# A pooled attention, a two-of-four expert layer and a gated convolution in one kernel: the tile of mixed heads by three products, and loads, scalings and key projections in another order

## The chip, the cores and the metric

The kernel runs on one NeuronCore of a Trainium2 chip. The metric is the device time of one execution in microseconds (us). Times of different runs of a kernel lie within a per cent here; the profile is of one execution.

## What is computed

Three layers, each in float32. The batch is 4, the sequence 1152, pooled to 576 query positions; 8 heads of 64.

```
q_pool = q.reshape(B, H, S // 2, 2, D).mean(axis=3)
scores = (1 / sqrt(D)) * q_pool @ k.transpose(0, 1, 3, 2)
attn   = softmax(scores)                      # sum + 1e-9
x      = (attn @ v)  as (B, 576, 512)

logits = x @ w_gate                           # 4 experts, the best 2 by softmax
for e in range(4):                            # causal attention of width 64 per expert
    a   = softmax(causal((1 / sqrt(64)) * (x @ wq[e]) @ (x @ wk[e]).T))
    out += weight_of_e * (a @ (x @ wv[e]) @ wo[e])

gate = sigmoid(causal convolution of 5 taps over out)
y    = (gate * (out @ w_val)) @ w_out
```

## The kernel before

**Numbers in two parts.** Where float32 accuracy is wanted of a product in the faster format F32R, an operand x is split into a high part, x rounded to F32R, and a low part, the rest. A product of two split operands needs high x high, low x high and high x low; low x low is left out. `THREE = ((0, 0), (1, 0), (0, 1))` lists these.

**Stage 1, the attention (the first 510 us or so).** The 16 pairs of heads (`pairs`) are worked through one after the other. A pair has two units; unit 0 has four tiles of 128 queries, unit 1 five. The fifth, the mixed tile, (2, 4) in `UNITS`, takes the last 64 queries of both heads at once. For tile m:
- `scores` (line 408): for each of three groups of 384 keys, products into the PSUM tile `s`. In an ordinary tile the stationary operand `qst` has the high parts of 64 query dimensions in the upper partitions and the low parts in the lower; `ka` and `kb` hold the keys of the two heads, each key's dimensions twice over the partitions, as high and as low parts. Two products then give all four terms. In the mixed tile the columns are 64 queries of head 0 and 64 of head 1, with zeros in the other head's place, so that four products per group are wanted: two heads by two parts.
- `rowmin` (413, VectorE), `expo` (419, ScalarE), and, two tiles later, `transp` (457, TensorE), whose results ScalarE and VectorE bring to `pt` (465, 467).
- `shares` (428 to 435): the reciprocals of the sums on VectorE, then their spreading to `rm` on GpSimd. At the end of a unit `av` (470 to 494) transposes `rm` (444, 446), makes the 36 value products (482), and multiplies (484); GpSimd splits the result (491, 487), and a DMA stores it to `x_d` (488).

Ahead of this, `load` fetches a pair's keys `kt`, queries `qt` and values `vn` (344 to 348), and `prep` works over a pair in four portions on GpSimd: the two queries of a pool are added (387, `qp`), the keys cast and subtracted into `hlk` (364, 365), the queries scaled, cast and subtracted (380 to 382). DMAs then move the parts to the partitions in which `scores` wants them (371 for keys, twelve per pair; 375 to 377 for queries, six).

The first pair has its own way in (`first`): its data are loaded twice over the partitions, and the splits are made in place (`kpart`, `qpart`, lines 521 to 530).

**What sets the order.** Everything is written out by hand: each engine runs its instructions in the order of the code. The loop over m calls, in a fixed pattern, `transp` of tile m - 2, `expo` of m, `scores` of m + 1 and one portion of `prep`. Work put on the list `late` is issued one tile later. All DMAs are issued by SyncE, in one queue, in that same order. Behind it in the loop run two generators as background work, from m = 5 on: `dense_weights` (decodes the last layer's weights, a chunk per unit) and `expert_weights` with `folded_weights` (one step per tile). They use VectorE, GpSimd and SyncE.

**Stage 2, the experts (510 to 725 us).** Steps (b, g, i): batch, pair of experts, tile of queries. Between the parts of a step a list `fill` of TensorE work is used up: projections of queries and keys (`proj`, 233), values and gates (`vgate`, 264), the mixing of results, the folding of the last weights (`fold`). `proj` makes queries first (w = 0), then keys (w = 1), two halves each; `move` then copies them to `qs` and `ks` (245 to 250). The convolution's taps (206, VectorE) ride along behind the portions of `fill`; `RD` says at which of five steps the first portion has a rider. **Stage 3** (from 725 us) makes the last products and the output. Its sigmoids need a table of ScalarE, which a dummy activation (`warm`, 951) loads beforehand.

## Time and profile before

| | |
|---|---|
| runs of the kernel | 808.44 us median of 3 (804.37 to 809.11) |
| the profiled execution | 807.51 us, its span 805.7 us |
| TensorE busy | 769.3 us, 95% of the span |
| VectorE, ScalarE, GpSimd busy | 542.0, 473.7, 310.6 us (67%, 59%, 39%) |
| moved by DMA | 134.50 MB, mean 167 GB/s |

The profile is read in stretches, since the stages have different limits. A row of the timeline gives the start and the length of some like instructions in a row, and in brackets how long the engine had been idle before them and what ended that. SPq is SyncE's queue of DMA issues; a row there is the issuing, not the transfer.

### The profile page before, as it was taken

Reading aid. Unit: us, or ns where it says so; the run is one execution under the profiler, and the core shown is the slowest. Engines: PE = TensorE matmul, PEld = TensorE weight load, DVE = VectorE, ACT = ScalarE, POOL = GpSimd, SP = SyncE. Lnnn points to the kernel's source line nnn. Section 1 sums busy time; section 2 is a strip of 40 time slices with the busy share of each in tenths; the row PEclk is TensorE's granted clock in tenths of the full one; section 3 lists DMA queues with packets and bytes.
Section 4 is the critical chain, followed back from the end, with each engine's and each line's share of the span. In section 5 each row is a group of like instructions: output and inputs, shape, how many; then the busy total and the mean of one; then the engine's idle time right before and its main releaser. Section 6 shows DMA issues by size and latency. Waiting matters only on the chain.

```text
span 805.7 us, 14797 instructions
## 1 busy us (share of the span) xinstructions
PE 769.3 (95%) x5348; PEld 627.6 (78%) x5348; DVE 542.0 (67%) x998; ACT 473.7 (59%) x1024; POOL 310.6 (39%) x420
## 2 busy tenths in 40 slices
PE   5889999989999999999999999998999999988998
PEld 4658778767787787787787787887988989877887
DVE  4547877886787777565566566335579899897740
ACT  5547656665676676676566567523455564647532
POOL 3555765757746636525435421112222222230000
PEclk9989999999999999999999999999999999999999
DMA  7778688678787677666565564156465364800112
GB/s 232 155 199 234 152 234 230 183 227 231 226 243 205 194 237 181 179 197 163 163 204 149 168 184 180 44 142 192 89 167 153 92 194 117 265 33 15 66 66 91
DMA packets 86296, 134.50 MB, mean 167 GB/s; under 512 B 21584, under 2 KB 58960, under 8 KB 86224
## 3 DMA queue, kind: packets, MB, share of 16 engines
q1 hardware_dynamic: 86224, 133.57, 58.8%
q8 instruction: 42, 0.69, 0.4%
q14 instruction: 30, 0.25, 0.1%
HBM read 53.37 MB, written 21.76 MB: 93 GB/s over the span
## 4 chain that ended last, share of the span: by engine, by line
PE 71%; DVE 10%; DMA 6%; ACT 4%; SPq 4%; POOL 3%; issue 2%; ACTq 0%; DVEq 0%; POOLq 0%
PE t L482 17%; PE s L408 16%; PE t L457 13%; PE a L233 6%; PE o L998 6%; PE a L264 4%; DVE nm L413 3%; ACT p L419 3%; PE a L788 3%; DMA xh<-x_d 2%; PE s L690 2%; PE a L655 2%; PE a L762 1%; DVE pt L467 1%; SPq L513 1%
## 5 line engine op out<-in xcount | busy, mean ns | idle before, releaser
L465 ACT ACTIVATE pt<-t 128x384 f32<-128x384 f32 x288 | 132.6, 489 | 132.5 <-PE t L457 131.3
L413 DVE TENSOR_REDUCE nm<-s 128x1 f32<-128x1152 f32 x144 | 194.1, 1348 | 23.7 <-PE s L408 17.5
L457 PE MATMUL t<-ident,p 128*128 128x128 f32 x1296 | 205.5, 278 | 2.5 <-ACT pt L465 2.4
L419 ACT ACTIVATE p<-s,nm 128x1152 f32<-128x1152 f32 x144 | 176.0, 1222 | 38.4 <-DVE nm L413 35.8
L457 PEld LDWEIGHTS t<-ident,p 128*128 128x128 f32 x1296 | 151.0, 141 | 43.4 <-issue 13.5
L482 PE MATMUL t<-pt,vn 128*64 128x320 f32 (+1 forms) x1152 | 149.2, 413 | 0.0
L408 PE MATMUL s<-ka,qst 128*128 128x384 f32 x480 | 128.5, 371 | 8.5 <-ACT ka L529 6.8
L408 PE MATMUL s<-kb,qst 128*128 128x384 f32 x480 | 132.4, 368 | 2.2 <-ACT p L419 1.5
L482 PEld LDWEIGHTS t<-pt,vn 128*64 128x64 f32 x1152 | 80.8, 138 | 55.9 <-issue 4.6
L467 DVE COPY pt<-t 128x384 f32<-128x384 f32 x144 | 80.3, 558 | 63.4 <-PE t L457 59.1
L408 PEld LDWEIGHTS s<-ka,qst 128*128 128x128 f32 x480 | 77.9, 193 | 16.7 <-ACT p L419 8.9
L726 POOL TENSOR_TENSOR p<-p,sm 128x512 f32<-128x512 f32 (+3 forms) x32 | 40.1, 1254 | 113.3 <-DVE sm L724 82.1
L408 PEld LDWEIGHTS s<-kb,qst 128*128 128x128 f32 x480 | 77.3, 191 | 5.4 <-ACT p L419 2.1
L484 DVE TENSOR_TENSOR xf<-t,rb 128x256 f32<-128x256 f32 (+1 forms) x32 | 14.7, 458 | 76.4 <-PE t L482 75.7
L233 PE MATMUL a<-xh,wqk 128*128 128x288 f32 x384 | 59.2, 304 | 2.5 <-DVE pt L740 2.1
L233 PEld LDWEIGHTS a<-xh,wqk 128*128 128x128 f32 x384 | 53.6, 191 | 4.3 <-DVE pt L740 2.5
L711 ACT ACTIVATE p<-s,nm 128x256 f32<-128x256 f32 (+3 forms) x64 | 33.0, 523 | 21.9 <-DVE nm L700 21.9
L365 POOL TENSOR_TENSOR hlk<-kt,hlk 128x384 fp32r<-128x384 f32 x45 | 45.4, 1008 | 1.0
L387 POOL TENSOR_TENSOR qp<-qt 128x576 f32<-128x576 f32 x15 | 21.3, 1418 | 56.9 <-DMA qt<-in_q_dram 52.9
L491 POOL CAST xt<-xf 128x256 fp32r<-128x256 f32 (+1 forms) x32 | 13.6, 424 | 76.5 <-DVE xf L484 76.5
L206 DVE SCALAR_TENSOR_TENSOR gp<-x,cw,gp 128x572 f32<-128x572 f32 (+3 forms) x48 | 40.7, 849 | 2.6 <-ACT gp L809 2.1
L433 POOL COPY rm<-rs 128x256 f32<-128x256 f32 x32 | 12.9, 404 | 67.9 <-PE t L457 45.9
(170 smaller groups left out, 1077.7 us busy)
## 6 DMA issues: line engine op xcount, KB each, us to landing
ka<-hlk SPq DMA_DIRECT2D x90, 192.0 KB, 3.2
kb<-hlk SPq DMA_DIRECT2D x90, 192.0 KB, 3.7
vn<-in_v_dram SPq DMA_DIRECT2D x16, 576.0 KB, 8.0
xh<-x_d SPq DMA_DIRECT2D x16, 576.0 KB, 6.8
k<-hl SPq DMA_DIRECT2D x32, 288.0 KB, 4.9
kt<-in_k_dram SPq DMA_DIRECT2D x15, 576.0 KB, 5.6
qt<-in_q_dram SPq DMA_DIRECT2D x15, 576.0 KB, 6.5
x_d<-xt SPq DMA_DIRECT2D x16, 320.0 KB, 4.0
```

Of the source, the lines that this page charges most:

```text
L206: dve.scalar_tensor_tensor(out=gp[:, n:], in0=x[:, 0:SQ - n], scalar=cw[:, m, c:c + 1], in1=gp[:, n:], op0=ALU.mult, op1=ALU.add)
L233: pe.matmul(ps[:, 0:HQ], lhsT=wqk[wi][:, t, cs], rhs=xh[:, t, xi, qsl], start=o == 0, stop=o == len(ops) - 1)
L365: late.append(lambda: pool.tensor_tensor(out=hlk[:, 1, gs], in0=kt[:, gs], in1=f(hlk[:, 0, gs]), op=ALU.subtract))
L408: pe.matmul(ps[:, 0:GW], lhsT=a, rhs=c, start=o == 0, stop=o == len(ops) - 1)
L413: dve.tensor_reduce(d["nm"], d["s"][:, :, 0:GW], axis=AX.XY, op=ALU.min)
L419: act.activation(d["p"], d["s"][:, :, 0:GW], AF.Exp, bias=d["nm"], scale=-1.0, accum_out=sums[(2 * n + u) % len(sums)][:, i:i + 1])
L457: pe.transpose(ps[:, j * P:(j + 1) * P], p[:, g, j * P:(j + 1) * P], ident)
L465: act.activation(dst, src, AF.Copy)
L467: dve.tensor_copy(dst, src)
L482: pe.matmul(ps[64 * h:64 * h + 64, 0:N], lhsT=vn[:, h, j, :], rhs=pt[:, j, h, :], start=j == 0, stop=j == C - 1)
L726: pool.tensor_tensor(out=pv, in0=pv, in1=sm[:, :, None].to_broadcast([P, 2, w]), op=ALU.mult)
L998: pe.matmul(ps[:, 0:w], lhsT=hl[xi][:, kt, t * P - a:(t + 1) * P - a], rhs=end3["wo3"][:, kt, wi, c:c + w], start=o == 0, stop=o == len(op ...
```

## The change

- The mixed tile's queries are put into a tile of their own, `last`: head 0's 64 dimensions in the upper partitions, head 1's in the lower, high and low parts side by side. Their partner is `hlk`, the keys of both heads as GpSimd splits them, which now has two buffers and stays until the tile is done. Three products per group are made, by `THREE`. For the first pair `hlk` and `last` are filled by DMAs (`wholek`, `wholeq`).
- `load` comes at tile (1, 1) instead of (1, 2), queries before keys; the values are loaded for themselves at (0, 3) of the pair before.
- The pooled queries are kept in `qt`; the attention's output tiles have one buffer for both units, and the values two.
- In the first pair the high parts of the later queries (`qhigh`) are made by GpSimd instead of ScalarE.
- The background work begins at m = 10 instead of 5.
- In stage 2 `proj` makes keys first. The first portion of every fifth step has no rider any more. `warm` is moved to the last value products.

```
-        return [(1.48, lambda w=w, hf=hf: half(w, hf)) for w in range(2) for hf in range(2)]
+        return [(1.48, lambda w=w, hf=hf: half(w, hf)) for w in (1, 0) for hf in range(2)]
...
-        v_p1 = s1.enter_context(tc.tile_pool(reuse_waits="tile", name="v1", bufs=3))
+        v_p1 = s1.enter_context(tc.tile_pool(reuse_waits="tile", name="v1", bufs=2))
-        x_p = s1.enter_context(tc.tile_pool(reuse_waits="tile", name="x", bufs=2))
+        x_p = s1.enter_context(tc.tile_pool(reuse_waits="tile", name="x", bufs=1))
+        hlk_p = s1b.enter_context(tc.tile_pool(reuse_waits="tile", name="hlk", bufs=2))
...
-            act.activation(pair[0][:, 4 * P + R64:], zero, AF.Copy)
-            act.activation(pair[1][:, 4 * P:4 * P + R64], zero, AF.Copy)
+            last = qpool.tile([P, 2, 2, R64], F32R, name=f"last{par}")
+            for h in range(2):
+                for i in range(2):
+                    act.activation(last[64 * h:64 * h + 64, i, 1 - h], zero[64 * h:64 * h + 64], AF.Copy)
...
         def load(n):
             b, hp = pairs[n]
+            qt = nat.tile([P, 2, SQ], F32, name="qt")
+            nc.sync.dma_start(qt, q[b, hp])
             kt = nat.tile([P, C * P], F32, name="kt")
             nc.sync.dma_start(kt, k[b, hp])
-            qt = nat.tile([P, 2, SQ], F32, name="qt")
-            nc.sync.dma_start(qt, q[b, hp])
-            vn = v_p1.tile([P, 2, C, D], F32, name="vn")
-            nc.sync.dma_start(vn, v[b, 2 * hp:2 * hp + 2].rearrange("h (p c) d -> p h c d", p=P))
+        def load_values(n):
+            b, hp = pairs[n]
+            vals[n] = v_p1.tile([P, 2, C, D], F32, name="vn")
+            nc.sync.dma_start(vals[n], v[b, 2 * hp:2 * hp + 2].rearrange("h (p c) d -> p h c d", p=P))
...
             def qmove():
-                for r in range(2):
-                    nc.sync.dma_start(f(qa[64 * r:64 * r + 64, 0:SQ]), f(hlq[0:64, r, :]))
-                    nc.sync.dma_start(f(qb[64 * r:64 * r + 64, 0:512]), f(hlq[64:128, r, 0:512]))
-                    nc.sync.dma_start(f(qb[64 * r:64 * r + 64, 512 + R64:]), f(hlq[64:128, r, 512:]))
+                for h in range(2):
+                    hs = slice(64 * h, 64 * h + 64)
+                    for r in range(2):
+                        nc.sync.dma_start(f(qst[n % 2][h][64 * r:64 * r + 64, 0:4 * P]), f(hlq[hs, r, 0:4 * P]))
+                    nc.sync.dma_start(f(qst[n % 2][2][hs, :, h]), f(hlq[hs, :, 4 * P:]))
...
-                ops = [(qs[hh][:, 4 * P:], ks[hh][:, s, g * GW:(g + 1) * GW]) for hh in range(2) for s in range(2)]
+                ops = [(qs[2][:, i].rearrange("p h q -> p (h q)"), kn[:, s, g * GW:(g + 1) * GW]) for i, s in THREE]
...
+            def qhigh(h, i):
+                a, z = cuts[i]
+                pool.tensor_scalar(qst[0][h][:, a:z], qd[h][:, 0, a:z], -scale / 2, None, op0=ALU.mult)
...
+            def wholek():
+                for h in range(2):
+                    nc.sync.dma_start(f(hlk[hs[h]]), f(kst[h][hs[h]]))
+
+            def wholeq():
+                for h in range(2):
+                    for i in range(2):
+                        nc.sync.dma_start(f(qst[0][2][hs[h], i, h]), f(qst[0][h][64 * i:64 * i + 64, 4 * P:]))
...
                 qadd(h, i, pool)
+                if i:
+                    qhigh(h, i)
...
-                if (u, i) == (1, 2) and n + 2 < len(pairs):
+                if (u, i) == (1, 1) and n + 2 < len(pairs):
                     load(n + 2)
-                if m == 5:
+                if (u, i) == (0, 3) and n + 1 < len(pairs):
+                    load_values(n + 1)
+                if m == 10:
...
+                if then is begin_last:
+                    act.activation(warm, zero[:, 0:1], AF.Sigmoid)
...
-        RD = (1, 0, 1, 1, 1)
+        RD = (0, 0, 1, 1, 1)
...
-            if n == len(steps) - 1:
-                act.activation(warm, zero[:, 0:1], AF.Sigmoid)
```

TensorE at the mixed tile of pair 0, before; L408 are score products, with the keys `ka`, `kb` of the two heads, L457 transposes of the tile two earlier.

```order
L457 MATMUL t<-ident,p 128x128 x6
L408 MATMUL s<-ka,qst_134 128x384 x2
L408 MATMUL s<-kb,qst_135 128x384 x2
L457 MATMUL t<-ident,p 128x128 x3
L408 MATMUL s<-ka,qst_134 128x384 x2
L408 MATMUL s<-kb,qst_135 128x384 x2
```

The same place in the changed kernel, with all three groups of keys, where the rows of before stop after two.

```order
L463 MATMUL t<-ident,p 128x128 x6
L414 MATMUL s<-hlk,last_139 128x384 x3
L463 MATMUL t<-ident,p 128x128 x3
L414 MATMUL s<-hlk,last_139 128x384 x6
L463 MATMUL t<-ident,p 128x128 x6
```

Nothing moved but the score products: three per group instead of four, with other operands.

SyncE's queue before, from the last key moves of pair 1 to the loads of pair 2; craw, wraw and wst are weights, x_d is the attention's output.

```order
L371 DMA ka<-hlk 64x2x384 x2
L371 DMA kb<-hlk 64x2x384 x2
L168 DMA craw<-in_moe_conv_w_dram 128x5x2 x4
L175 DMA wraw<-in_moe_w_val_dram 128x512
L127 DMA wst<-in_moe_wq_dram 128x4x64
L344 DMA kt<-in_k_dram 128x1152
L346 DMA qt<-in_q_dram 128x1152
L348 DMA vn<-in_v_dram 128x2x576
```

The same queue in the changed kernel, from the values of pair 1 on.

```order
L355 DMA vn<-in_v_dram 128x2x576
L376 DMA ka<-hlk 64x2x384 x2
L376 DMA kb<-hlk 64x2x384 x2
L549 DMA last_139<-qst_137 64x64 x2
L549 DMA last_139<-qst_138 64x64 x2
L376 DMA ka<-hlk 64x2x384 x2
L376 DMA kb<-hlk 64x2x384 x2
L347 DMA qt<-in_q_dram 128x1152
L349 DMA kt<-in_k_dram 128x1152
```

The weights are gone from in front of the loads, the first pair's pieces of `last` and the values have come, and queries go out before keys.

SyncE's queue at the start of the experts before, with the second expert pair's queries and keys and the next batch's input `xh`.

```order
L247 DMA q_6189<-hl 64x576
L249 DMA q_6190<-hl 64x512
L250 DMA q_6190<-hl 64x64
L900 DMA xh<-x_d_68 128x1152 x2
L245 DMA k_6193<-hl 64x1152
L245 DMA k_6194<-hl 64x1152
L245 DMA k_6193<-hl 64x1152
L245 DMA k_6194<-hl 64x1152
L900 DMA xh<-x_d_68 128x1152 x2
```

And in the changed kernel.

```order
L245 DMA k_6147<-hl 64x1152
L245 DMA k_6148<-hl 64x1152
L925 DMA xh<-x_d_68 128x1152 x2
L247 DMA q_6143<-hl 64x576
L249 DMA q_6144<-hl 64x512
L250 DMA q_6144<-hl 64x64
L247 DMA q_6143<-hl 64x576
L249 DMA q_6144<-hl 64x512
L250 DMA q_6144<-hl 64x64
L925 DMA xh<-x_d_68 128x1152 x2
```

The four key moves have gone ahead of the six query moves; the input stays around what comes second.

## Rows read from the trace of the kernel before

**Rows 1.** Busy time by stretch; columns: stretch and length, busy (count) per engine, granted clock, DMA.
```profile
50.00:58.00 8.00, 8.00 (x39) 3.91 (x38) 0.00 (x0) 1.64 (x3) 5.11 (x6) 0.65 0.70 171
58.00:182.00 124.00, 120.14 (x852) 94.39 (x852) 97.42 (x152) 80.90 (x151) 79.81 (x120) 1.00 0.74 206
182.00:514.00 332.00, 330.49 (x2363) 258.42 (x2359) 219.55 (x314) 217.00 (x407) 153.14 (x207) 1.00 0.66 189
```

**Rows 2.** The chain that ended last, in the steady part; columns: start, length, what.
```profile
211.54 5.00 PE t L482 x36
...
326.21 1.39 PE s L408 x8
```

**Rows 3.** Timeline behind a mixed tile of the steady part.
```profile
358.44 1.36 DVE L413 TENSOR_REDUCE nm<-s 128x1 f32<-128x1152 f32 x1 [0.86 <-PE s L408]
358.77 0.87 ACT L465 ACTIVATE pt<-t 128x384 f32<-128x384 f32 x2 [0.73 <-PE t L457]
```

**Rows 4.** TensorE's waits, 0 to 60 us; columns: total us, times, longest.
```profile
PE t L457 <- ACT pt L465: 2.1, 2, 1.6
```

**Rows 5.** Timeline, 28 to 62 us.
```profile
29.12 1.28 SPq L371 DMA_DIRECT2D ka<-hlk  x2
...
35.20 3.11 SPq L168 DMA_DIRECT2D craw<-in_moe_conv_w_dram  x4
...
39.39 0.51 SPq L344 DMA_DIRECT2D kt<-in_k_dram  x1
...
46.45 1.40 POOL L387 TENSOR_TENSOR qp<-qt 128x576 f32<-128x576 f32 x1 [4.18 <-DMA qt<-in_q_dram]
...
49.42 0.69 PE L444 MATMUL t<-ident,rm 128*128 128x128 f32 x2 [3.16 <-POOL rm L433]
...
50.62 7.53 PE L482 MATMUL t<-pt,vn 128*64 128x320 f32 x36
```

**Rows 6.** Timeline, 8 to 23 us, VectorE and GpSimd.
```profile
8.07 1.03 DVE L530 TENSOR_TENSOR ka<-pt,ka 128x384 fp32r<-128x384 f32 x2 [1.68 <-ACT ka L529]
...
8.57 1.12 POOL L517 TENSOR_TENSOR pt<-pt 128x256 f32<-128x256 f32 x1 [4.64 <-DMA pt<-in_q_dram]
...
14.62 1.01 POOL L517 TENSOR_TENSOR pt<-pt 128x256 f32<-128x256 f32 x2 [0.75 <-DMA pt<-in_q_dram]
...
19.29 1.41 POOL L387 TENSOR_TENSOR qp<-qt 128x576 f32<-128x576 f32 x1 [3.66 <-DMA qt<-in_q_dram]
...
20.65 0.50 POOL L364 CAST hlk<-kt 128x384 fp32r<-128x384 f32 x1
...
22.33 1.65 POOL L380 TENSOR_SCALAR qp<-qp 128x576 f32<-128x576 f32 x1
```

**Rows 7.** The 15 query loads, line 346: from issue to landing.
```profile
DMA to landing us min/median/max: 5.6/6.5/7.7
```

**Rows 8.** TensorE's waits, 60 to 200 us.
```profile
PE t L444 <- POOL rm L433: 3.0, 2, 2.2
```

**Rows 9.** Timeline, 542 to 560 us: VectorE, SyncE's queue and TensorE.
```profile
542.45 0.81 DVE L216 SCALAR_TENSOR_TENSOR hl<-a,hl 128x288 fp32r<-128x288 f32 x2
...
546.39 3.89 SPq L245 DMA_DIRECT2D k<-hl  x4
550.32 1.62 SPq L900 DMA_DIRECT2D xh<-x_d  x2
...
555.87 0.47 PE L690 MATMUL s<-k,q 128*128 128x256 f32 x2 [3.26 <-DMA k<-hl]
...
559.44 1.09 PE L233 MATMUL a<-xh,wqk 128*128 128x288 f32 x3 [0.16 <-DMA xh<-x_d]
```

**Rows 10.** Timeline at the end of the experts.
```profile
723.57 1.28 ACT L951 ACT_TABLE_LOAD   x1
...
725.51 0.41 PE L762 MATMUL a<-ident,p 128*128 128x128 f32 x2 [0.82 <-ACT q L738]
```

**Rows 11.** Timeline, GpSimd's shares in the steady part.
```profile
363.24 0.40 POOL L433 COPY rm<-rs 128x256 f32<-128x256 f32 x1 [4.61 <-PE t L457]
```

More of the change, by code (lines that the diff above doesn't have):

```diff
@@ L318, in tile_kernel @@
         for par in range(2):
-            pair = [qpool.tile([P, 4 * P + 2 * R64], F32R, name=f"qst{par}{h}") for h in range(2)]
-            act.activation(pair[0][:, 4 * P + R64:], zero, AF.Copy)
-            act.activation(pair[1][:, 4 * P:4 * P + R64], zero, AF.Copy)
-            qst.append(pair)
+            qst.append([qpool.tile([P, SQ], F32R, name=f"qst{par}{h}") for h in range(2)])
+            last = qpool.tile([P, 2, 2, R64], F32R, name=f"last{par}")
+            for h in range(2):
+                for i in range(2):
+                    act.activation(last[64 * h:64 * h + 64, i, 1 - h], zero[64 * h:64 * h + 64], AF.Copy)
+            qst[par].append(last)
         sums = [sums_p.tile([P, 5], F32, name=f"sums{i}") for i in range(3)]
@@ L398, in scores @@
             n, u, i, (h, t) = tiles[m]
-            qs, ks, vn = data[n]
+            qs, ks, kn = data[n]
             if g == 0:
@@ L471, in av @@
             b, hp = pairs[n]
-            vn = data[n][2]
+            vn = vals.pop(n) if u else vals[n]
             pt = pts.pop((n, u))
@@ L504, in first @@
             kd, qd = bufs[0:2], [t.rearrange("p (r q) -> p r q", r=2) for t in bufs[2:4]]
-            vn = v_p1.tile([P, 2, C, D], F32, name="vn")
             kst = [kst_p.tile([P, 2, C * P], F32R, name=n) for n in ("ka", "kb")]
-            data[0] = [qst[0], kst, vn]
+            hlk = hlk_p.tile([P, 2, C * P], F32R, name="hlk")
+            data[0] = [qst[0], kst, hlk]
             cuts = [(0, Q0), (Q0, 4 * P), (4 * P, SQ)]
```

29 lines of the change are left out of this document (14 added, 15 removed).

## The prediction

> **What bounds the kernel now.** I read four views: the busy times by stretch, the list of what TensorE waited for, the chain that ended last, and the timeline around each wait. The stretches show two regimes [rows 1]. From 182 to 514 us, in the later eleven pairs of the attention, TensorE is busy for 330.5 of 332 us at full clock: nothing but its own work sets the time. [...] So the change is to be priced twice, as TensorE work in the steady part and as waits at the start and in the tail.
>
> **The mixed tile.** Every pair has one tile that takes the last 64 queries of both heads. It has four products for each of three groups of keys, now three: one product less per group, 3 x 16 = 48 of 960 score products. Eight of them in a row take 1.39 us on the chain [rows 2], so one costs 0.174 us where TensorE never stops (a single row shows more, since neighbours overlap). That is 0.522 us per pair. Is another engine behind it? VectorE's reduction of just this tile had been idle 0.86 us for TensorE, and ScalarE's next eviction 0.73 us [rows 3], both more than 0.52, so they follow. Pair 0 does not count, as a wait comes behind it (below). **15 x 0.522 = 7.8 us.** Bounds: 0, if the next tile waits in its place, and 8.35 with pair 0. The products read the two-head keys straight from GpSimd's tile, so a copy is no longer in front of them; the second buffer of that tile lets GpSimd write the next pair beside it. I cost this at nothing.
>
> **The start, to the first pair's second value product.** Two waits of TensorE: 2.1 us for ScalarE's evictions [rows 4], and 3.16 us at 49.42 us for GpSimd's shares, behind which the 36 value products took 7.53 us [rows 5], at the low clock of rows 1. In the steady part the same 36 take 5.00 us [rows 2]: 2.5 us more.
> - ScalarE loses two pairs of scalings that stand in front of its evictions. What this gives lies within the 2.1 us of rows 4, and ahead of the wait below, which swallows it. Eight small clears instead of four stand before its first data, and hide behind the first loads.
> - GpSimd gets four multiplications. By 1.65 us for 576 columns [rows 6] they are 0.73, 0.18, 0.73 and 0.18, together 1.8 us. Its adds end at 15.6 us, so it is free at 17.4, before the 19.29 us at which it now begins on the next pair's queries. Free, as long as the cover of 1.9 us holds; without it, what is over is late in the same chain.
> - That pair's queries are now issued ahead of its keys. The keys then land about where the queries did (19.29 us), and the cast of the keys, now at 20.65, can start up to 1.3 us sooner. GpSimd runs on behind it without a gap to the first shares; I take 1.2 us.
> - Then the wait at 49.42 us. SyncE's queue is full from 22 us on. Before the next loads, whose keys now go out at 39.39 us [rows 5], it loses four small weight DMAs (3.11 us) and two weight loads (0.51 each, as the key load), 4.1 us, and gets two whole-key copies, four query pieces (0.64 each, half of the 1.28 for two key moves) and the values (0.51), 4.4 us. This nearly cancels. What is left is 0.9 of the 1.2 us from above: queries issued at 38.5 us, the place of the keys, and keys at 39.0. Second in line, a load lands 5.6 to 7.7 us later, the median being 6.5 [rows 7]: 45.5 us. Behind that stand the cast (0.50, rows 6) and the shares (0.40, rows 11): TensorE starts at 46.4 instead of 49.4, **3.0 us** sooner. It will want them at 49.42 - 3.16 - 1.2 - 0.52 = 44.5, so a wait of 1.9 us is left. After a wait of 2.2 us later in the run [rows 8] the granted clock stayed at 1.00 [rows 1]; so the low clock should not come, and **2.5 us** go too. Together 5.5 us; this holds the 1.2 us and pair 0's 0.52. Bounds: 0.6 us (the slowest landing, 1.2 us later, SyncE 1.2 us later, and the low clock still there) and 7.8 (the waits of rows 4 and 5 and the clock all gone).
>
> [...] GpSimd's first add took 1.12 us for 256 columns while VectorE subtracted from two tiles in SBUF, and the last two, of 256 and 64, took 1.01 together [rows 6]. [...]
>
> **Loads a tile sooner, background work five tiles later.** Between 60 and 200 us TensorE waited 3.0 us for the shares, twice [rows 8], as GpSimd had stood in front of them waiting for queries, which at 46.45 us [rows 5] it did for 4.18 us. The loads now go ahead of a weight load and of the value products of that tile, and queries ahead of keys. The queue is full, so this is two or three issues at 0.5 us and one load, not a tile; still more than most of these waits. **2.5 us** of 3.0. Bounds: 3.0 gone, or one more wait of 2.2 us, since the weights' work meets the pairs in a new phase. Values with two buffers are written a pair ahead, and the product that frees them lies two tiles back: nothing. One buffer less for the attention's output has a unit of four or five tiles to empty: nothing.
>
> **The experts.** With keys first the wait of 3.26 us for the last keys [rows 9] is met, as they are issued 3.5 us sooner. But right behind it TensorE waits for the next batch's input until 559.44 us, 9.1 us after the second half of it began to be issued. SyncE's instructions there are the same, only reordered: keys from 542.9, when the first of the two subtractions of rows 9 ends (0.4 after 542.45), 3.9 us; half of the input, 1.6 at most; six queries at 0.64; the other half from 552.2 instead of 550.32. It begins sooner and ends later, with the same bytes. I take **0.4 us**; bounds -1.9 and +3.3. The skipped first rider moves VectorE's taps behind an eviction, and none goes: 0, with 1 us allowed either way. The table load for the last sigmoids (1.28 us, with TensorE idle for 0.82 behind it [rows 10]) moves behind the last value products' first part, where ScalarE idles: **0.8 us**, bounds 0 and 1.3.
>
> **Sum.** 7.8 + 5.5 + 2.5 + 0.4 + 0.8 = 17.0 us off the profiled execution's 807.5 us (span 805.7 and 1.8 around it, which stays) makes 790.5. That execution lies 0.9 us below the median of the runs shown; against that median it would be 791.4. I say 791.0 us.
>
> **Rivals.**
> - *All waits go.* For it: the loads no longer compete with weights. Against it: SyncE's queue is as full. 8.35 + 7.8 + 3.0 + 1.3 + 3.3 = 23.8: 783.7 us.
> - *The early waits stay.* For it: keys now land last, and the cast in front of the shares needs them; the whole-key copies take the place of the weights in the queues. Then 7.8 + 0.8 + 0.4: 798.5 us.
> - *Another engine takes over in the mixed tile.* ScalarE and VectorE work almost as long in a tile as TensorE. Against it: rows 3. Then the 7.8 are lost: 798.3 us.
> - *Slower.* At every pair GpSimd stands at the cast until the keys land, now second, and the shares come late. Place: the cast of rows 6, fifteen times. In the steady part GpSimd is 4.61 us ahead when it comes to the shares [rows 11], so keys would have to land 4.6 us later before it costs anything, and from 17.0 / 15 = 1.1 us beyond that the change loses. At 2 us beyond: 15 x 2 = 30, and the 2.5 lost: 807.5 + 30 - 14.5 = 823.0 us.
>
> **How the numbers follow.** Forecast 0.58 (its own range 786 to 795), all waits go 0.15, early waits stay 0.17, another engine 0.07, slower 0.03. The range of 784 to 799 leaves out half of the first rival, the slower one and some at the edges. A measurement of this kernel can tell about 1%, 8 us, from no change: the border is 800.4 us. Forecast and first rival lie below it; so do most of the two near 798, of which I give a quarter (0.06) to no change. Faster 0.91, same 0.06, slower 0.03.
>
> **What would show it.** In the changed profile: 912 score products instead of 960, and each steady pair 0.5 us shorter than now, with TensorE still over 99% busy (right), or idle times behind the mixed tile (the third rival). The shares near 46 us, and a granted clock of 1.00 behind them, or again 7.5 us for 36 products. GpSimd's wait for queries short, with a new one for keys. No wait for keys at the experts' start, and one for the input in its place. The prediction is wrong if the steady pairs keep their length, or if shares are waited for in the steady part.

## The result and the profile after

Predicted 791.0 us (784 to 799, faster with 0.91). Measured: 813.5 us (median of 7, 812.5 to 817.8) against 804.8 us before (median of 7, 801.7 to 809.1), ratio 1.0114 with a 95% interval of 1.0089 to 1.0138. The change makes the kernel about 1.1% **slower**.

The profiled execution took 813.0 us (span 811.2; before 807.5 and 805.7). That of the kernel before lies 2.7 us above its median of 7, so the two traces differ by 5.5 us and not by the 8.7 between the medians; it is these 5.5 us that the traces can explain. Busy time by stretch, as [rows 1]:

```profile
50.00:58.00 8.00, 7.97 (x59) 5.49 (x59) 4.07 (x7) 5.08 (x9) 6.18 (x7) 1.00 0.39 99
58.00:182.00 124.00, 117.57 (x830) 90.99 (x826) 93.58 (x144) 79.48 (x148) 72.55 (x113) 1.00 0.79 209
182.00:514.00 332.00, 326.94 (x2322) 252.16 (x2323) 226.94 (x326) 216.00 (x406) 162.94 (x218) 0.99 0.68 193
```

From 50 to 58 us the granted clock is 1.00 now (0.65 before), but from 58 to 182 us TensorE is idle for 6.4 us instead of 3.9. To find where the time went, I follow one instruction through both traces: VectorE's write of the attention output (xf) at the end of a pair. First before, then after (timeline, VectorE): end of the first pair, of the sixth, of the last.

```profile
58.27 0.49 DVE L484 TENSOR_TENSOR xf<-t,rb 128x320 f32<-128x320 f32 x1 [8.88 <-PE t L482]
216.66 0.49 DVE L484 TENSOR_TENSOR xf<-t,rb 128x320 f32<-128x320 f32 x1 [0.84 <-PE t L482]
530.77 0.49 DVE L484 TENSOR_TENSOR xf<-t,rb 128x320 f32<-128x320 f32 x1 [6.34 <-PE t L482]
```
```profile
58.75 0.49 DVE L490 TENSOR_TENSOR xf<-t,rb 128x320 f32<-128x320 f32 x1 [4.14 <-PE t L488]
224.40 0.49 DVE L490 TENSOR_TENSOR xf<-t,rb 128x320 f32<-128x320 f32 x1 [4.67 <-PE t L488]
533.96 0.49 DVE L490 TENSOR_TENSOR xf<-t,rb 128x320 f32<-128x320 f32 x1 [6.38 <-PE t L488]
```

| stretch | before, us | after, us | difference | predicted |
|---|---|---|---|---|
| to the end of the first pair | 58.3 | 58.8 | +0.5 | -5.5 |
| five pairs beside the weights' work | 158.4 | 165.7 | **+7.3** | -5.1 (2.5 and five mixed tiles) |
| the other ten pairs | 314.1 | 309.6 | -4.6 | -5.2 |
| the rest | 274.9 | 277.2 | +2.3 | -1.2 |

(The last row runs to the span's end.) "First pair" and "five pairs" below mean the first two rows.

**The mixed tile did what was forecast.** On the chain of waits, six of its nine products take 1.05 us, and a steady pair lasts 30.33 us (310.48 less 280.15) where it took 30.77 before (303.88 less 273.11). First before, then after:

```profile
273.11 5.00 PE t L482 x36
...
303.88 5.00 PE t L482 x36
```
```profile
272.02 1.05 PE s L414 x6
280.15 5.00 PE t L488 x36
...
302.36 1.05 PE s L414 x6
310.48 5.00 PE t L488 x36
```

**The start has a new wait.** Timeline, SyncE's queue and TensorE; below it the DMA issues from 20 to 46 us (count, KB of each, median us to landing):

```profile
24.31 0.55 SPq L544 DMA_DIRECT2D hlk<-ka  x1
24.96 0.84 SPq L544 DMA_DIRECT2D hlk<-kb  x1
25.89 4.29 SPq L382 DMA_DIRECT2D qst<-hlq  x2
...
37.35 2.91 SPq L549 DMA_DIRECT2D last<-qst  x4
...
42.38 1.30 PE L414 MATMUL s<-hlk,last 128*128 128x384 f32 x3 [5.83 <-DMA last<-qst]
...
42.99 0.60 SPq L347 DMA_DIRECT2D qt<-in_q_dram  x1
```
```profile
hlk<-ka SPq DMA_DIRECT2D x1, 576.0 KB, 5.5
hlk<-kb SPq DMA_DIRECT2D x1, 576.0 KB, 7.5
...
last<-qst SPq DMA_DIRECT2D x4, 16.0 KB, 3.6
```

The wait for the shares at 49.42 us and the 7.53 us of low clock behind it [rows 5] are gone. In their place TensorE stands 5.83 us earlier on, for the four small copies of the first pair's last queries, and has a granted clock of 0.50 from 40 to 44 and 0.65 from 44 to 48 us. These copies are issued at 37 us, since they come late in SyncE's program, and SyncE stood 4.29 us at the second pair's queries behind two whole-key copies of 576 KB each; without the copies (pair0, below) the same two issues took 1.81 us. The small copies, of 16 KB each, took 2.7 to 4.4 us from issue to landing; what stood ahead of them in that time is not shown.

**In the five pairs TensorE waits again and again**: 9.3 us in 11 waits, 8.1 of them for the shares, where it was 3.3 us in three. Its waits after (us in total, times, longest):

```profile
PE t L450 <- POOL rm L439: 7.2, 6, 2.4
PE t L488 <- DVE pt L473: 1.2, 2, 0.7
PE t L452 <- POOL rm L441: 0.9, 3, 0.5
```

So of the 7.3 us that the five pairs lost, the waits make 6.0 and a stretch of low clock behind the last of them, from 217 to 221 us, 1.7 (none before); five shorter mixed tiles take 2.2 off, and what is left is in waits too short for the list. One of the waits, with GpSimd and SyncE before it:

```profile
72.78 0.59 SPq L347 DMA_DIRECT2D qt<-in_q_dram  x1
73.41 0.78 SPq L349 DMA_DIRECT2D kt<-in_k_dram  x1
74.29 2.11 SPq L127 DMA_DIRECT2D wst<-in_moe_wq_dram  x2
...
81.46 0.40 POOL L136 CAST wqk<-wst 128x256 fp32r<-128x256 f32 x1 [5.46 <-DMA wst<-in_moe_wq_dram]
81.81 1.42 POOL L393 TENSOR_TENSOR qt<-qt 128x576 f32<-128x576 f32 x1
...
84.31 0.39 POOL L439 COPY rm<-rs 128x256 f32<-128x256 f32 x1
...
84.76 0.44 PE L450 MATMUL t<-ident,rm 128*128 128x128 f32 x2 [1.22 <-POOL rm L439]
```

GpSimd stands for a piece of weights that was issued behind 1.15 MB of queries and keys; the pair's query sum and the shares' copies stand behind that piece. GpSimd's main waits for DMAs in the five pairs, before and after:

```profile
POOL qp L387 <- DMA qt<-in_q_dram: 17.3, 4, 5.1
POOL qp L387 <- DMA x_d<-xt: 4.1, 1, 4.1
POOL wvg L136 <- DMA wst<-in_moe_w_gate_dram: 2.4, 2, 1.8
```
```profile
POOL xt L497 <- DMA x_d<-xt: 8.7, 4, 3.0
POOL wqk L136 <- DMA wst<-in_moe_wq_dram: 5.5, 1, 5.5
POOL qt L393 <- DMA qt<-in_q_dram: 5.3, 3, 3.5
POOL wvg L136 <- DMA wst<-in_moe_wv_dram: 5.2, 1, 5.2
POOL wqk L136 <- DMA wst<-in_moe_wk_dram: 3.1, 2, 1.7
```

The wait for queries shrank by 12 us, and others took its place: pieces of weights (`wst`), and the output's store (`x_d<-xt`), which must have read its one buffer before GpSimd writes the next output there.

**The experts' start** waits as long as before, now for queries (3.83 us; before 3.26 for keys [rows 9], and 0.49 right behind for which the profile shows no releaser), but the low clock behind it lasts longer. Windows, first before, then after; the granted clock is the third number from the end:

```profile
556.00:560.00 4.00, 3.35 (x15) 2.83 (x16) 1.21 (x3) 0.00 (x0) 0.61 (x1) 0.68 0.61 236
560.00:564.00 4.00, 4.00 (x27) 3.81 (x26) 1.73 (x6) 2.00 (x7) 0.74 (x1) 0.90 0.00 0
```
```profile
556.00:560.00 4.00, 0.38 (x2) 0.41 (x2) 2.94 (x11) 1.25 (x6) 1.72 (x2) 0.85 1.07 261
560.00:564.00 4.00, 4.00 (x17) 3.74 (x17) 1.12 (x2) 0.00 (x0) 0.04 (x1) 0.50 0.47 188
564.00:568.00 4.00, 4.00 (x24) 3.79 (x23) 1.60 (x6) 2.00 (x7) 0.92 (x1) 0.80 0.00 0
```

Four microseconds times what is missing to 1.00: 1.7 us before, 3.4 after. A part of it falls while TensorE still stands; weighted with the busy time of each microsecond, 1.6 us are lost before and 3.0 after.

### The profile page after: what moved, and what is told of

It reads as the page before. It is cut to its first block, busy times and chain, and to the rows that moved or that the text cites. A ratio compares the mean times of both kernels' runs of the same rounds, so it can differ in the third digit from the quotient of the medians.

```text
span 811.2 us, 14745 instructions
## 1 busy us (share of the span) xinstructions
PE 766.6 (94%) x5300; PEld 623.3 (77%) x5300; DVE 547.6 (68%) x998; ACT 474.0 (58%) x1024; POOL 314.4 (39%) x424
## 4 chain that ended last, share of the span: by engine, by line
PE 66%; DVE 9%; DMA 9%; POOL 6%; SPq 4%; issue 4%; ACT 3%; POOLq 0%; ACTq 0%; DVEq 0%
PE t L488 15%; PE s L414 13%; PE t L463 11%; PE a L233 6%; PE o L1021 6%; PE a L264 4%; PE a L813 3%; DVE nm L419 2%; ACT p L425 2%; PE s L713 2%; DMA xh<-x_d 2%; PE a L678 2%; SPq L376 2%; DMA qt<-in_q_dram 2%; PE a L785 1%
## 5 line engine op out<-in xcount | busy, mean ns | idle before, releaser
L463 PEld LDWEIGHTS t<-ident,p 128*128 128x128 f32 x1296 | 152.1, 142 | 42.7 <-issue 13.5
L414 PE MATMUL s<-kb,qst 128*128 128x384 f32 x384 | 109.0, 380 | 1.2 <-ACT p L425 1.1
L414 PE MATMUL s<-ka,qst 128*128 128x384 f32 x384 | 101.6, 374 | 8.5 <-ACT ka L539 6.8
L414 PEld LDWEIGHTS s<-ka,qst 128*128 128x128 f32 x384 | 62.5, 193 | 16.4 <-ACT p L425 8.6
L414 PEld LDWEIGHTS s<-kb,qst 128*128 128x128 f32 x384 | 60.8, 194 | 4.7 <-ACT p L425 1.6
L497 POOL CAST xt<-xf 128x256 fp32r<-128x256 f32 (+1 forms) x32 | 13.6, 425 | 83.5 <-DVE xf L490 67.2
L414 PE MATMUL s<-hlk,last 128*128 128x384 f32 x144 | 34.6, 368 | 5.8 <-DMA last<-qst 5.8
L439 POOL COPY rm<-rs 128x256 f32<-128x256 f32 x32 | 12.9, 404 | 65.5 <-DVE rs L435 57.6
```

The lines of the kernel that those rows point to most:

```text
L414: pe.matmul(ps[:, 0:GW], lhsT=a, rhs=c, start=o == 0, stop=o == len(ops) - 1)
L463: pe.transpose(ps[:, j * P:(j + 1) * P], p[:, g, j * P:(j + 1) * P], ident)
```

## The experiments

Eighteen kernels, each compared with the kernel before in the same session (its median there 804.1 to 805.6 us). The first-pair and five-pair times are of one profiled execution each, and executions of one kernel spread by 2 to 12 us, so differences of 1 us between traces say little. "Waits" are TensorE's in the five pairs; the low clock behind them is not in it. The two columns of pairs trade with each other (bg5 gives back 4.1 us in one and loses 3.8 in the other), so their sum, the end of the sixth pair, is the safer measure (216.7 us before, 224.4 changed).

| kernel | median, us | ratio (interval) | first pair | five pairs | waits |
|---|---|---|---|---|---|
| before | 804.8 | 1 | 58.3 | 158.4 | 3.3 |
| changed | 813.5 | 1.0114 (1.0089, 1.0138) | 58.8 | 165.7 | 9.3 |
| x2 | 816.9 | 1.0128 (1.0106, 1.0150) | 58.3 | 165.6 | 8.4 |
| bg5 | 816.7 | 1.0134 (1.0103, 1.0165) | 62.6 | 161.6 | 4.4 |
| pair0 | 810.9 | 1.0068 (1.0046, 1.0091) | 51.3 | 168.9 | 9.1 |
| qfirst | 813.8 | 1.0105 (1.0081, 1.0130) | 58.7 | 166.8 | 8.7 |
| load12 | 813.1 | 1.0109 (1.0084, 1.0135) | 58.6 | 165.5 | 6.4 |
| order_old | 820.2 | 1.0189 (1.0166, 1.0212) | 67.2 | 164.2 | 6.8 |
| vals11 | 815.5 | 1.0135 (1.0103, 1.0166) | 58.1 | 167.0 | 8.9 |
| qp_own | 816.2 | 1.0141 (1.0105, 1.0176) | 57.6 | 165.2 | 8.1 |
| old_load11 | 807.4 | 1.0034 (1.0016, 1.0053) | 55.6 | 158.4 | 2.5 |
| old_bg10 | 804.0 | 0.9994 (0.9978, 1.0010) | 54.2 | 158.2 | 2.9 |
| old_v03 | 810.7 | 1.0087 (1.0053, 1.0121) | 60.2 | 159.3 | 2.5 |
| wst4 | 810.2 | 1.0075 (1.0048, 1.0102) | 59.0 | 160.3 | 4.3 |
| rm_dve | 811.8 | 1.0097 (1.0067, 1.0127) | 60.3 | 155.3 | 0.5 |
| pair0_vals11 | 810.1 | 1.0063 (1.0033, 1.0093) | 51.0 | 166.0 | 7.5 |
| pair0_rm_dve | 805.3 | 1.0010 (0.9984, 1.0036) | 50.1 | 159.0 | 4.3 |
| pair0_sched_old | 808.5 | 1.0048 (1.0027, 1.0068) | 58.3 | 160.1 | 4.4 |
| best | 804.0 | 0.9997 (0.9976, 1.0018) | 49.6 | 156.5 | 2.2 |
| best_ends_old | 803.1 | 0.9983 (0.9955, 1.0011) | 50.8 | 155.0 | 0.9 |

### The first pair's copies

```diff
+ pad0 = qpool.tile([P, 2, 2, R64], F32R, name="pad0")
+     act.activation(pad0[:, h, 1 - h], zero, AF.Copy)
...
+ elif n == 0:
+     ops = [(pad0[:, hh].rearrange("p h q -> p (h q)"), ks[hh][:, s, g * GW:(g + 1) * GW]) for hh in range(2) for s in range(2)]
...
- return {0: lambda: (qpart(1, 0), kpart(1, 0)), 1: lambda: (kpart(1, 1), kpart(1, 2), late.append(wholek)),
-         2: lambda: (qpart(0, 1), qpart(0, 2)), 3: lambda: (qpart(1, 1), qpart(1, 2), late.append(wholeq))}
+ return {0: lambda: (qpart(1, 0), kpart(1, 0)), 1: lambda: (kpart(1, 1), kpart(1, 2)),
+         2: lambda: (qpart(0, 1), qpart(0, 2)), 3: lambda: (qpart(1, 1), qpart(1, 2))}
```

> The changed kernel with the first pair's mixed tile by four products from two zero-padded tiles of queries, as before, so that neither its whole keys nor its queries are copied by SyncE (6 DMAs fewer in the first 41 us); all other pairs with three products. Theory: TensorE's 5.8 us for 'last' at 42 us is a loss of the copies' place in SyncE's queue. Then this wait is gone, the granted clock of 40 to 60 us comes back to 0.95 or more, and at the value products near 53 us the kernel is 5 to 8 us earlier. Of this the end gets all (ratio 1.001 to 1.005) if the later stages only follow the start. Rival: the next wait, for the shares at the end of the first pair, or GpSimd's work for the second pair, which comes by the same queue, takes over, as in the kernel before (1.9 us there and the low clock with it): gain at 58 us 0 to 3 us, ratio 1.008 to 1.012.

```profile
23.93 1.81 SPq L385 DMA_DIRECT2D qst<-hlq  x2
...
36.26 0.60 SPq L350 DMA_DIRECT2D qt<-in_q_dram  x1
...
45.15 0.44 PE L455 MATMUL t<-ident,rm 128*128 128x128 f32 x2
...
46.11 5.07 PE L493 MATMUL t<-pt,vn 128*64 128x320 f32 x36
```

Shown: without the copies the next queries are issued at 36.26 instead of 42.99 us, TensorE finds the shares at 45.15 us without a wait, and no low clock shows (six transposes in 0.82 us at 42.95 us, where the changed kernel took 1.19 behind its wait; 36 products in 5.07 us). The first pair ends 7.4 us sooner. The end gets about half of it (ratio 1.0068), as the five pairs take 3.2 us longer.

### One part undone, or done alone

The output's buffer:

```diff
- xt = x_p.tile([P, 2 * (256 + R64)], F32R, name="xt")[:, 0:2 * N].rearrange("p (i n) -> p i n", i=2)
+ xt = x_p.tile([P, 2, N], F32R, name=f"xt{u}")
```

> The changed kernel with one buffer of 'xt' for each unit of a pair instead of one for both (xf stays one). Theory A, the single output buffer: its store in DRAM is late in SyncE's queue, GpSimd stands 16.2 us at the cast of 'xf' in 6 waits, the background's weight work and the pair's query sum behind it come late, and TensorE waits for the copies of the shares (7.2 us in 6 waits from 60 to 217 us, where the kernel before lost 3.0 from 60 to 200). Then GpSimd's waits for x_d<-xt are gone, those of TensorE for rm from 60 to 217 us fall to 3 us or less, the stretch at a lower clock near 217 us goes, and the time falls by 4 to 7 us, to a ratio of 1.002 to 1.007 over the kernel before. Rival B, the background's start five tiles later: GpSimd's waits for x_d<-xt go, but TensorE still waits 6 to 8 us for rm and the ratio stays at 1.010 to 1.013.

```profile
PE t L450 <- POOL rm L439: 7.1, 4, 2.9
```

GpSimd's waits for the store are gone, TensorE's for the shares are not: theory A falls. GpSimd now stands for pieces of weights at the same places (from 60 to 250 us, 8.5 us for wq and 7.4 for wv).

The background's start and the loads:

```diff
- if m == 10:
+ if m == 5:
...
- if (u, i) == (1, 1) and n + 2 < len(pairs):
+ if (u, i) == (1, 2) and n + 2 < len(pairs):
```

The first edit is bg5, the second load12; old_bg10 and old_load11 make the reverse of each in the kernel before.

> The changed kernel with the background work begun at the sixth tile again instead of the eleventh. Theory A, the single output buffer: nothing or a little worse, ratio 1.009 to 1.015, TensorE still loses 6 us or more for rm from 60 to 217 us. Rival B, the later start: those waits fall to about 3 us as before, and the time falls by 4 to 7 us, ratio 1.002 to 1.007. The start is as in the changed kernel by both (5.8 us for 'last' in the first pair).

> The changed kernel with a pair's queries and keys loaded at the second unit's third tile again, not its second. Measure: from the output 'xf' of the first pair's second unit to that of the sixth's (five pairs): 158.4 us in the kernel before, 165.7 in the changed one, 151.7 at five steady pairs of 30.33. Theory C, the place of the loads: a piece of weights (wst) that is issued behind the 1.15 MB of qt and kt lands 7 us later, GpSimd stands at its cast with the pair's query sum and the shares' copies behind it, and TensorE waits for the shares and then runs at a lower clock; a tile earlier puts the loads in front of that piece. Then the five pairs take 155 to 160 us and the ratio falls to 1.002 to 1.007. Rival D, the phase of the weights' pieces alone: five pairs take 163 to 168, ratio 1.010 to 1.014.

> The kernel before with one change, its loads (keys, queries, values) at the second unit's second tile instead of the third. Theory C: TensorE's waits for the shares from 60 to 217 us grow from 3 to 6 us or more, five pairs take 162 us or more (158.4 before, 153.9 at a steady 30.79), ratio 1.004 to 1.010. Prediction's theory (a tile sooner ends the waits): five pairs 155 to 157, ratio 0.995 to 0.999.

> The kernel before with one change, the background's start at the eleventh tile instead of the sixth. Prediction's theory: the first pair's wait for the shares (1.9 us and a lower clock of about 2.5 us) goes, since the weights' first DMAs are no longer in front of the second pair's queries: the output of the first pair's second unit comes 3 to 5 us earlier, five pairs take 157 to 160, ratio 0.993 to 0.998. Theory D, the phase of the weights' pieces: the first pair gains as much, but five pairs take 162 us or more, ratio 0.999 to 1.006.

Neither is it. With bg5 the five pairs give back 4.1 us and the first pair loses 3.8, so that the sixth pair ends where it did; load12 gives nothing. In the kernel before, both edits leave the five pairs as they were (158.4 and 158.2), and the first pair gains 2.7 and 4.0 us in the traces. The timed runs do not bear out a gain: old_bg10 is level, and old_load11 loses 0.3% (its trace is of the fastest of its 12 executions, 804.4 to 810.8, and that of the kernel before lies above its median). So the prediction's reading of the first pair fits the traces of the kernel that it was read from, and is not shown in its time.

What a load's place does can be seen too. In old_load11 the queries are issued 0.1 us after the output of the pair's first unit, in the mean of the five pairs, where the kernel before issues them 1.6 us after it: 1.5 us sooner, about the "two or three issues and one load" of the prediction.

Place of the values, the sum in place, and the old schedule:

```diff
- if (u, i) == (0, 3) and n + 1 < len(pairs):
+ if (u, i) == (1, 1) and n + 1 < len(pairs):
      load_values(n + 1)
...
- qp = qt[:, 0]
+ qp = nat.tile([P, SQ], F32, name="qp")
```

The first edit is vals11 (old_v03 loads the values at (0, 3) in the kernel before), the second qp_own. pair0_vals11 has pair0's edit too. order_old has both edits of bg5 and load12, and loads kt ahead of qt.

> The changed kernel with a pair's values loaded right behind the next pair's queries and keys (second unit's second tile) instead of at the first unit's fourth tile. Measure as before: five pairs from the first pair's last 'xf', 158.4 us in the kernel before, 165.7 in the changed one, 151.7 if steady. Theory V, the values' place: 576 KB now stand in front of the key pieces that SyncE sends in the first unit (their landing went from 3.2 and 3.7 us to 5.2), SyncE comes later to the output's store and to qt and kt, and GpSimd's query sum with the shares behind it is late. Then the pieces land in 3 to 4 us again, qt is issued 1.5 us or more sooner in its pair, five pairs take 154 to 160 us, ratio 1.000 to 1.007. Rival F, what is left of the structure (query sum in place, one output buffer, kept keys): five pairs 163 us or more, ratio 1.009 to 1.014.

> The kernel before with one change, a pair's values loaded at the first unit's fourth tile of the pair before it instead of with its keys and queries. Theory V: key pieces land 1 to 2 us later, five pairs take 162 us or more (158.4 before), TensorE's waits for the shares from 60 to 217 us rise from 3 to 6 us or more, ratio 1.004 to 1.012. Rival F: five pairs 156 to 160, ratio 0.997 to 1.002.

> The changed kernel with the sum of a pair's queries in a tile of its own again, not in place in qt. Theory G: qt is held until its low part is made, so the next pair's load, and SyncE with it, stand for GpSimd; then SyncE's issue of qt comes 1 us or more sooner in its pair, and five pairs take 155 to 161 us, ratio 1.001 to 1.007. Theory V and the others: qt is free long before its load is issued; five pairs 163 to 168 us, ratio 1.010 to 1.014.

> Both: the first pair's mixed tile by four products without SyncE's copies, and the values loaded behind the next pair's queries and keys. Theories of the start and V: the first pair's last 'xf' comes 6 to 8 us sooner than in the changed kernel, five pairs take 154 to 160 us, and the time is below that of the kernel before, ratio 0.990 to 0.998. If V is not it: 1.004 to 1.009, as with the first pair alone (1.0068).

> The changed kernel with place and order of the pair's loads (keys, then queries, at the second unit's third tile) and the background's start (sixth tile) as in the kernel before; the values stay a load of their own at the first unit's fourth tile. If the schedule of the background and the loads is what costs (theories C and D together), the five pairs take 154 to 158 us after the start, and the ratio is 1.000 to 1.005 with the start's loss of 4 to 5 us in it. Rival E: what the new structure itself brings (query sum in place in qt, so that qt is held till its low part is made; one output buffer; keys hlk held for the mixed tile) costs: five pairs 162 us or more, ratio over 1.008.

All fell in the changed kernel. The values' new place costs the kernel before 0.9% (old_v03), though not in the five pairs; putting them back in the changed kernel (vals11) gives no time. There the queries are issued 1.4 us sooner than in the changed kernel, but 1.7 MB then stand in front of the pieces of weights, and GpSimd's two longest waits for these are 8.2 and 7.0 us. order_old ends its first pair 8.9 us behind the kernel before, with waits of 8.8 us for the shares and 4.2 for the copies, and still takes 164.2 us for the five pairs.

### What GpSimd stands for, and who waits for GpSimd

```diff
- st = bufs[j] = raws.tile([P, DM], F32, name="wst")[:, 0:width]
+ st = bufs[j] = wst_p.tile([P, DM], F32, name=f"wst{j % 4}")[:, 0:width]
...
- fetch(j + 1)
+ fetch(j + 2)
...
- pool.tensor_copy(rm[:, 0:2].rearrange("p t (h d) -> p t h d", d=D), both)
+ dve.tensor_copy(rm[:, 0:2].rearrange("p t (h d) -> p t h d", d=D), both)
```

The first two edits are wst4 (the folded weights alike), the last, with the scaling below it, rm_dve.

> The changed kernel with the experts' and folded weights' pieces (wst) in four buffers of their own and fetched two pieces ahead instead of one in two buffers. Theory C in its sharper form: GpSimd stands at the cast of a piece whose load was issued behind qt and kt (5.5, 5.2 and 3.1 us from 58 to 225 us). Then GpSimd's waits for wst fall from 17 us to under 5, TensorE's waits for rm from 60 to 225 us from 7.2 to under 4, five pairs take 156 to 161 us, ratio 1.001 to 1.007. If the piece is only one of several DMAs that come late (x_d, qt), another of them takes its place: five pairs 163 us or more, ratio 1.009 to 1.014.

GpSimd's and TensorE's waits in the five pairs of wst4:

```profile
POOL qt L396 <- DMA qt<-in_q_dram: 15.0, 5, 4.8
...
POOL xt L500 <- DMA x_d<-xt: 10.6, 3, 6.1
...
POOL wqk L137 <- DMA wst<-in_moe_wq_dram: 0.9, 1, 0.9
```
```profile
PE t L453 <- POOL rm L442: 3.7, 2, 2.6
```

The waits for weight pieces are nearly gone, and with them 5.3 of the 7.3 us that the five pairs had lost. Queries and the store are waited for more, but less of that reaches TensorE. By this trace it is the largest part that removing one of the causes gives back there with the first pair as it was; the timed runs show 1.0075 instead of 1.0114, with intervals that overlap.

> The changed kernel with the copies of the shares (rm) made by VectorE, right behind the reciprocal, instead of GpSimd. Theory H: whatever makes GpSimd late (a weight piece that lands behind qt and kt, the output's store, the query load itself), TensorE loses time only because the shares' copies stand in GpSimd's queue behind it. Then TensorE's waits for rm (7.2 us in 6 waits from 60 to 225 us) and the low clock behind them are gone, five pairs take 153 to 157 us (165.7 in the changed kernel, 151.7 steady), the start's loss stays, ratio 0.998 to 1.004. Rival I: the second unit's shares wait is only the first of several; with it gone TensorE stands for the pair's keys and queries, which come from the same GpSimd queue 10 us later: waits for ka, kb or qst of 4 us or more appear, five pairs take 161 us or more, ratio 1.008 to 1.013.

```profile
PE t L450 <- DVE rm L439: 0.5, 1, 0.5
```

Theory H holds in the five pairs: with the shares made by VectorE they take 155.3 us, 10.4 less, at a granted clock of 1.00, and no wait for keys or queries appears. So what the five pairs had lost passed through the shares' copies, which stand in GpSimd's queue behind all that it waits for. The time gained less than that: in this execution the first pair's wait for the copies was 8.1 us instead of 5.8, and in the ten later pairs the VectorE copies take back the mixed tile's gain (the ten pairs take 314.6 us, 309.6 in the changed kernel).

> Shares' copies by VectorE and the first pair's mixed tile by four products without SyncE's copies. Theories of the start and H: the first pair's last 'xf' comes 6 to 8 us sooner than in the changed kernel and five pairs take 153 to 157 us; ratio 0.988 to 0.996. Rival I: ratio 1.002 to 1.008.

> The changed kernel with the first pair as in pair0 and with place and order of loads and background as in the kernel before (keys, queries, then values at the second unit's third tile, background from the sixth). What is left of the change is then the mixed tile by three products in seven pairs, the sum in place, one output buffer and the order of the experts. If the schedule of loads and background together makes the loss, five pairs take 153 to 158 us and the ratio is 0.990 to 0.997, the mixed tile's 3.5 to 7 us below the kernel before. If the structure (one output buffer, kept keys) makes it, five pairs take 162 us or more, ratio 1.003 or more.

The first is 8 us below the changed kernel by the medians and level with the kernel before, so the copies of the first pair and the shares behind GpSimd together are of the size of the loss. It missed its own forecast of a gain: the five pairs take 159.0 us, with 1.3 us for keys among the waits, and the ten later pairs 317.2.

The second has loads, values and background as in the kernel before. Its five pairs take 160.1 us, 8.8 less than pair0's, but it lost in its first pair what pair0 gains (3.4 us of wait for query pieces and 2.7 for the shares), and the sixth pair ends less than 2 us sooner than pair0's. So the old schedule mostly moves the loss.

### The experts, and all together

```diff
- return [(1.48, lambda w=w, hf=hf: half(w, hf)) for w in (1, 0) for hf in range(2)]
+ return [(1.48, lambda w=w, hf=hf: half(w, hf)) for w in range(2) for hf in range(2)]
```

This is qfirst; best_ends_old also takes back RD and the place of the table load.

> The changed kernel with the experts' queries projected ahead of their keys, as before. Theory: keys first ends the wait of the first expert scores later, for the queries' 6 DMAs come last (3.8 us of wait for q against 3.3 for k in the kernel before); undone, the time falls by 0.3 to 1.0 us, ratio 1.010 to 1.011. Rival, the prediction's: keys first gains 0.4; undone, the ratio is 1.0115 to 1.0125. A difference under 1 us will be seen in the stage's own rows alone.

> The changed kernel with four things: the first pair's mixed tile by four products (no copies by SyncE), the shares' copies by VectorE, the weight pieces in four buffers fetched two ahead, and one xt buffer for each unit. If the losses found so far (the start's copies; GpSimd's lateness by weight pieces, output buffer and loads, which TensorE sees by the shares) are all of it up to 515 us, the first pair ends 7 to 8 us before the changed kernel, five pairs take 153 to 156 us (159.0 with the first two of these things alone), and the ratio is 0.992 to 0.998. If the waits of GpSimd for the output's store and the weights no longer matter once the shares are VectorE's, the five pairs stay at 158 to 160 and the ratio at 0.999 to 1.003.

> The same with the three edits of the experts' part undone: queries ahead of keys, the table load at the last step, the rider list as before. Theory K, these edits cost: the changed kernel loses 2.3 us more from 531 us to its end (lag 3.2 to 5.5), by waits for xh of 1.5 us instead of 0.4, for VectorE's pt of 2.2 instead of 1.3, and 0.5 more at the first expert scores. Then this kernel is 1 to 3 us faster than the one beside it, ratio lower by 0.001 to 0.004, waits for xh 0.5 or less and for pt 1.3. Rival, the prediction's 1.2 us of gain by them: it is 1 us slower, ratio higher by 0.001 to 0.002. Rival L: what is lost there is the clock's, by the phase alone: within 0.5 us, the waits for xh as in the other.

best is pair0, rm_dve, wst4 and x2 in one; best_ends_old undoes the three edits of the experts' part. Their five pairs take 156.5 and 155.0 us, and their first pair ends 8.7 and 7.5 us ahead of the kernel before. So the losses of the attention are found, though undoing them costs VectorE's copies. By 531 us best is 9.4 us ahead; 5.1 of that are lost again behind it. TensorE's waits for the experts' input there, best and best_ends_old (0.4 us in the kernel before):

```profile
PE a L235 <- DMA xh<-x_d: 2.5, 4, 0.8
```
```profile
PE a L235 <- DMA xh<-x_d: 1.2, 2, 0.7
```

The two differ by 1.0 us, within their intervals, so the edits of the experts' part are neither shown to cost nor to gain. qfirst against the changed kernel says the same. No version here beats the kernel before by more than the measurement can tell.

## Why the prediction was wrong

- **Mixed tile (7.8 us):** right. 0.44 us a pair on the chain instead of 0.52, 4.6 of 5.2 us in the ten pairs, and VectorE and ScalarE followed: TensorE's listed waits in these pairs are 0.3 us in both kernels.
- **Start (5.5 us):** wrong by 6. The failed step is "two whole-key copies, four query pieces (0.64 each ...)": the copies were priced by what SyncE needs to issue them. They carry 576 KB each, the queue stood behind them (4.29 us for the next two issues), and the mixed tile of the first pair had to wait 5.83 us for the last piece of that queue. "This nearly cancels" was wrong by 4.5 us (42.99 instead of 38.5 for the queries), and the wait of the mixed tile was not looked for: I had said that a copy is "no longer in front" of these products, which holds for all pairs but the first. Without the copies (pair0) no low clock shows there (six transposes in 0.82 us, not 1.19), and the shares stand ready at 45.15 us. That this lies near the forecast 46.4 is luck: by the same sum, less the 3.8 us for six copies, it would be 42.6. The queries went out at 36.26 instead of 34.7 us, and GpSimd's sum of them (1.42 us) stood behind their landing, not the keys that the sum counted last. The 1.2 us for the earlier cast were 0.6 to 0.7 (cast at 19.97, first shares at 28.59, 29.21 before). Eight clears, the four multiplications and their cover held: GpSimd began the second pair's queries at 18.62 us (19.29 before). Its multiplications took 2.8 us together, where the estimate by columns gave 1.8: 1.19 and 0.85 us for 256 columns (0.73 each), 0.37 twice for 64 (0.18 each).
- **Loads and background (2.5 us):** wrong, 7.3 us the other way with the mixed tiles in it. The forecast was that the loads come "two or three issues at 0.5 us and one load" sooner, and that the waits then go. In the five pairs of before, queries are issued -0.3 to 2.5 us after the output of the pair's first unit, 1.6 in the mean; after the change 0.7 to 2.1, 1.4 in the mean: only 0.2 us sooner. The step holds for the move alone (1.5 us sooner in old_load11); what took it back, by vals11, is the values' load, which now stands ahead in the same queue and was priced at its issue of 0.51 us: with the values behind the loads the queries come 1.4 us sooner. But sooner queries did not help either: five pairs take 167.0 us in vals11. The shares' copies begin 11.8 to 13.2 us after that output (mean 12.3) where they began at 10.2 to 13.5 (11.5), while TensorE, with shorter pairs, wants them at 11.5 instead of 11.9. The step that failed is the wait: the sum counted the one for queries as the only thing in front of the shares. Of its 17.3 us 12 went, as forecast, but pieces of weights behind the larger loads, and the output's store, stood there instead. The bound "one more wait of 2.2 us" was too narrow by far.
- **"Nothing" for the output's buffer and the values:** the store's waits are real (8.7 us on GpSimd), but undoing this part alone changes nothing. The values' place is not nothing: alone it costs the kernel before 0.9% (old_v03).
- **Low clock:** "After a wait of 2.2 us the clock stayed at 1.00" was carried over as if the length of one wait decided. In the changed kernel it stayed at 1.00 behind a wait of 2.39 us near 150 us, and was 0.72 from 216 to 222 us behind one of 1.36 and one of 0.47 us.
- **The experts (1.2 us):** nothing gained, 2.3 lost in the trace: clock +1.4 (weighted with the busy time), waits for the input +1.1, for VectorE's eviction +0.9, for the first scores +0.1, against 1.2 for ScalarE's eviction and 0.35 for the table load that went; this accounts for 2.0 of the 2.3. Keys first moved the wait to the queries (3.83 us, where it was 3.26 for keys), as their move is the last of the queue.
- **The rivals:** none was it. "The early waits stay" came nearest to the start: it named the whole-key copies in the queue, but took the old wait to stay and not a new one to come. The slower one had GpSimd stand for the keys; it stands for weights and stores.

Still open: which single edit starts the loss in the five pairs. None of those that undo one edit gives it all back, and the three tried in the kernel before do not make it. What is shown is the way it takes (GpSimd's queue, then the shares) and, in the traces, its largest part (pieces of weights behind the loads). The waits for the experts' input (0.8 to 2.6 us with the changed attention, 0.4 before) were not followed to their cause.

## What to carry to other kernels

Here a copy between tiles cost its bytes in the queue, not only its issue: two copies of 576 KB took 1.39 us to issue, and the two issues behind them 4.29 us instead of 1.81. So before a DMA is put in front of something that is waited for, add up the KB that then stand ahead. Where a result stands behind several waits of one engine, the question is not how long one wait is, but which DMA lands last among all that stand ahead of the result, and how much cover that result has. Here it had about none (TensorE wanted the shares 11.5 us after the output of the pair's first unit, and their copies began 12.3 us after it in the mean), and a DMA wait removed was replaced by the next: in the five pairs GpSimd's waits for queries fell from 17.3 to 5.3 us, and those for pieces of weights rose from 4.2 to 17.5. And a load that was moved up in the program came sooner by about what it overtook in its queue, 1.5 us in old_load11, but another load put ahead of it took this back (0.2 us were left in the changed kernel).

## What the runs showed of the hardware

- The same wait at the experts' start, 3.3 to 5.0 us, cost 1.7 or 1.8 us of clock in some kernels and 3.4 in others, whichever of keys or queries it was for (for keys: before 1.7, old_bg10 3.4; for queries: rm_dve 1.8, changed 3.4).
- Two issues of 128 KB each took SyncE 4.29 us right behind two copies of 576 KB each between tiles, and 1.81 us without these (pair0).
- The median of the mean granted clock is 0.985 in the changed kernel's 7 runs and 0.992 in the 95 of the kernel before from all comparisons. 0.007 of 811 us is 5.7 us, so of the 8.7 us between the medians up to this much may be the clock behind the waits and not the waits themselves; this is an estimate, and some of it falls while TensorE stands. In the two profiled executions what is missing to full clock is 8.5 and 6.8 us, 1.7 of the 5.5 us between them.
